# A long convolution and a spectral mix on one core: slot order and copying engines at the borders of pairs, a product from PSUM, and the place of one load

## The chip, the cores and the metric

The kernel runs on one core of a Trainium2 chip. The time is device time of one execution, in microseconds (us). Engines: TensorE (PE) multiplies matrices and writes to PSUM; VectorE (DVE) and ScalarE (ACT) compute on SBUF and PSUM and copy between them; GpSimd (POOL) here issues DMAs and clears memory; SyncE (SP) issues DMAs. PSUM has eight banks of 512 32-bit words a partition.

## What is computed

```python
def _attn_ref(x, h):                      # x: 8 x 5696 x 128, h: 5696 x 128
    L = 2 * S
    y = irfft(rfft(x, n=L, axis=1) * rfft(h, n=L, axis=0)[None], n=L, axis=1)[:, :S]
    return y

def _moe_ref(x, w_r, w_i, w_ch):          # x is y of above; w_r, w_i: 64 x 128 x 128
    X = rfft(x, axis=1)
    # the first 64 modes are multiplied by complex 128 x 128 matrices, the others are dropped
    u = x + irfft(Y, n=S, axis=1)
    return u + maximum(u @ w_ch, 0)
```

The result is 8 x 5696 x 128 in float32. The first function is a causal convolution along the sequence; the second mixes the channels of the 64 lowest modes, adds the result and ends in a channel matmul with relu.

## The kernel before, in words

A transform of length 2 x 5696 is taken apart as 64 x 178. The kernel has 90 frequencies k of the inner transform (NK), done four at a time: 23 **ticks** (NT), the last with two. The eight batches go in four **pairs** (NP, `g_` from 0 to 3). There are two blocks. Block one transforms, multiplies with the filter and transforms back half-way, writing `zscr` in HBM; it also sums the spectrum's 64 modes in PSUM bank 7 (`MB`). Block two reads `zscr` again (tiles ZT0 to ZT4), finishes the convolution, adds the mixed modes and writes the output.

A recorder (lines 21 to 121) keeps one list of instructions an engine, in the order of the Python code. Each engine runs its list in order, so the order of the code is the order of each queue; the recorder derives the semaphore waits from tokens such as `("bank", 3)`, `("as", 12)` or `("u", 0)`.

**Start.** PE first transforms the filter h in 16 tiles (lines 409 to 423). Between their matmuls stand fillers, which multiply the constant F1 with itself into banks 6 and 7 and whose result nobody reads: four behind each tile, twelve behind the last (line 416). DVE meanwhile spreads x into `x_sb` (named Xin; `x_place`, line 355).

**Tiles of x.** `a_tile(j)` (line 429), j from 0 to 31, is the first transform of one pair: four matmuls with F1 (128x180) into two banks (a **slot**, named by its first bank), then a copy of 128x720 into `a_sb` (As), by DVE or ACT. All 32 tiles must be copied before the next pair's first tick (`AST`, line 427). For pair 0 they run ahead of the ticks; for the others, tiles 0 to 6 stand in the last four ticks of the pair before (`border`, line 508, with slot and engine of each), and tiles 7 to 31 behind them (lines 633 and 634), in slots 2, 0, 4, 6 by a counter that runs on from pair to pair, the copies by DVE and ACT in turn. Eight fillers follow the last one (`keep`, line 636).

**Ticks.** `tick(g_, t)` (line 556), t from 0 to 25, has in this order: the Xin copies of the next pair on DVE (ticks in `XPLACE`, line 551); 16 matmuls of As with the twiddles M into slot 0 or 2, alternating by tick (lines 563 to 571); the product with the filter (`products`, line 535); the border's tiles; the issue on POOL of a load of x for the next pair, Xt (even ticks 2 to 16, line 576), which waits for U of that tick; with the U of two ticks before (LC), four matmuls with Wc, two ACT copies into Zs or Zt and the write to `zscr` on SP (lines 579 to 594); with the Z of three ticks before (LM), the sums of modes in bank 7 (matmuls with G, lines 595 to 610). In pair 0 a part of the filter's transform is in the tick too.

A product (line 547, DVE, 128x2048 into U) reads its spectrum either from a copy that ACT made (Xs, line 544), which takes 1.22 us on DVE, or straight from PSUM, which takes 2.28 us and holds the two banks until then. Line 542 chooses: in pairs 1 to 3 the ticks 2, 5, ... 20 read from PSUM.

Behind a pair's last tick, ACT copies the mode sums out of bank 7 in two pieces (XT, lines 628 to 631).

**Ahead of block two.** In pair 3, some ticks issue the loads of block two on POOL (`early`, line 509). Behind tick 21 (NT - 2) stand, in this order: ZT1 (two DMAs, which wait for writes to `zscr` through tick 14, `SLACK`), the constant IBs, a memset of a part of ZT1, ZT2, a memset of ZT2. Each waits also for the tick's U (`pace`). Behind the pair come WI, ZT3 and ZT4 with their memsets.

**Block two** (from line 648). PE needs IBs and C (the mixed modes) to finish its first tile. It takes the ZT tiles in turn; when one has been used, SP loads the next into it.

Of the kernel before, what the change touches and what calls it, by code (L numbers as in the profile page):

```python
# [4 lines left out]
P = 128  # L5
# [118 lines left out]
def bass_long_conv_fft__then__afno_spectral_mix_kernel(nc, x, h, moe_w_r, moe_w_i, moe_w_ch, out):  # L124
    B, S, D = x.shape
# [170 lines left out]
    def bank(i):  # L296
        return ("bank", i)
# [111 lines left out]
    for j in range(16):  # L409
        t = turns("h", [0, 2, 4])  # L410
        for i in range(4):
            d = 4 * j + i
            mm(pv(t + i // 2, (i % 2) * 2 * NK, [[1, 2 * NK]]),
               ap(hp_sb, 2 * J * HS, 0, P, d, [[HS, 2 * J]]), f1_sb[:, :], True, True,
               [("hz",), ("hp", d // DC), ("f1",)], [bank(t + i // 2)])
        for i in range(4 if j < 15 else 12):
            mm(pv(6 + i % 2, 0, [[1, 2 * NK]]), f1_sb[:, 0:P], f1_sb[:, :], True, True, [("f1",)], [bank(6 + i % 2)])
        evac(bass.AP(ah_sb, 4 * j, [[HW, P], [DH, 2 * NK], [2, 2], [1, 2]]),
             pv(t, 0, [[1, 2 * NK], [512, 2], [2 * NK, 2]]),
             [bank(t), bank(t + 1)], [("ah", j)], 1.0 / 64,  # L420
             eng="vector" if j % 4 == 3 else "scalar")
        if j % 2:
            x_place(j // 2, x_raw[j // 2], XR[j // 2])

    HP = [("hz",), ("hp", 0), ("hp", 1)]
    AHT = [("ah", j) for j in range(16)]
    AST = [("as", j) for j in range(32)]

    def a_tile(j, slots, eng=None):
        t = turns("s", slots) if len(slots) > 1 else slots[0]  # L430
        for i in range(4):
            d = 4 * j + i
            mm(pv(t + i // 2, (i % 2) * 2 * NK, [[1, 2 * NK]]),
               ap(x_sb, XW, 0, P, d, [[XS, 2 * J]]), f1_sb[:, :], True, True,
               XIN + XZ + [("f1",)], [bank(t + i // 2)])
        evac(bass.AP(a_sb, 4 * j, [[AW, P], [D, 2 * NK], [2, 2], [1, 2]]),
             pv(t, 0, [[1, 2 * NK], [512, 2], [2 * NK, 2]]),
             [bank(t), bank(t + 1)], [("as", j)], 1.0 / 64, eng=eng, after=once(("hp", j), HP))
# [63 lines left out]
    def load_s4(part):  # L502
# [2 lines left out]
            [("s4", part, 0)], after=pace + (AST if part else M_ALL[1:4]))  # L505

    V, A = "vector", "scalar"
    border = {NT - 1: [(0, 2, V)], NT: [(1, 0, V), (2, 2, A)], NT + 1: [(3, 0, V), (4, 2, A)], NT + 2: [(5, 0, V), (6, 2, V)]}
    early = {0: lambda: load_id(), 1: lambda: load_w(0), 3: lambda: load_w(1), 6: lambda: load_w(2), 8: lambda: load_w(3),
             12: lambda: load_s4(1), 16: lambda: load_s4(0),  # L510
             14: lambda: clear_zt(0),
             15: lambda: load_zt(0, "gpsimd"),
             NT - 2: lambda: (load_zt(1, "gpsimd", SLACK), load_ib(), clear_zt(1), load_zt(2, "gpsimd"), clear_zt(2))}
    pace = []
    SLACK = [("zd", NP - 1, s_) for s_ in range(NT - NZL)]

# [18 lines left out]
    def products(g_, t, sl):  # L535
        n = len(ticks[t])
        bk = [bank(sl), bank(sl + 1)]
        i = t % NU
        hv = bass.AP(h_sb, KT * t * D, [[2 * HW, P], [HW, 2], [0, 2], [1, n * D]])
        uv = bass.AP(u_s[i], 0, [[2048, P], [1024, 2], [512, 2], [1, n * D]])  # L540
        src = pv(sl, 0, [[0, 2], [512, 2], [1, n * D]])
        if t % 3 != 2 if g_ else t != NT - 4:
            e = turns("e", list(range(NXS)))
            evac(bass.AP(x_s[e], 0, [[1024, P], [512, 2], [1, n * D]]), pv(sl, 0, [[512, 2], [1, n * D]]), bk,
                 [("xs", e)], eng="scalar")
            src, bk = bass.AP(x_s[e], 0, [[1024, P], [0, 2], [512, 2], [1, n * D]]), [("xs", e)]
        R.add("vector", lambda e: e.tensor_tensor(uv, src, hv, MULT),  # L547
              bk + [("h", t, 0), ("h", t, 1, 0), ("h", t, 1, J)], [("u", i)])
# [7 lines left out]
    def tick(g_, t):  # L556
        if g_ + 1 < NP:
            for i in range(2 * XC):
                if t == XPLACE[g_ > 0][i]:
                    x_place(i, x_st[i], xtok(i))  # L560
        with_h = with_h_at(g_, t)
        if t < NT:
            sl = XSLOT[0] if with_h else XSLOT[(t + (g_ == 0)) % 2]
            for i, k in enumerate(ticks[t]):
                for r in range(2):
                    for b in range(2):
                        col = k * 3 * J + (J if r == 0 else 0) + b * J
                        mm(pv(sl + b, i * D, [[1, D]]),
                           ap(m_sb, MW, J * b, J, col, [[1, P]]),
                           ap(a_sb, AW, J * b, J, (2 * k + r) * D, [[1, D]]), r == 0, r == 1,  # L570
                           AST + mtok(k), [bank(sl + b)])
            products(g_, t, sl)
        if t in border and g_ + 1 < NP:
            for j, sl, e in border[t]:
                a_tile(j, [sl], e)
        if g_ + 1 < NP and t % 2 == 0 and 0 < t <= 4 * XC:
            i = t // 2 - 1
            x_load(g_ + 1, i, x_st[i], xtok(i), [("u", t % NU)] + AST)
        if LC <= t < NT + LC:
            s_ = t - LC  # L580
            n = len(ticks[s_])
            i, zi = s_ % NU, s_ % NZS[g_]
            zb = [turns("z", ZBANK) for b in range(2)]
            for b in range(2):
                for r in range(2):
                    mm(pv(zb[b], 0, [[1, n * D]]), (W1, W2)[r], u_s[i][:, r * 1024 + b * 512:r * 1024 + b * 512 + n * D],
                       r == 0, r == 1, [("u", i), ("wc",)], [bank(zb[b])])
                evac(bass.AP(z_s[zi], b * D, [[1024, P], [2 * D, n], [1, D]]),
                     pv(zb[b], 0, [[D, n], [1, D]]), [bank(zb[b])], [("zs", zi, b)], eng="scalar",
                     after=once(("zx", zi, b), Z_OLD) if zi >= NZ else ())  # L590
            zo = (g_ * NK + KT * s_) * P * 256
            dma("sync", bass.AP(zs, zo, [[256, P], [P * 256, n], [1, 256]]),
                bass.AP(z_s[zi], 0, [[1024, P], [256, n], [1, 256]]), "z",
                [("zs", zi, 0), ("zs", zi, 1)], [("zd", g_, s_)])
        if LM <= t < NT + LM:
            s_ = t - LM
            zi = s_ % NZS[g_]
            if s_ == 0:
                mm(pv(MB, 0, [[1, 2 * P]]), m_sb[ZR:P, 0:P], ap(f1_sb, 2 * NK, ZR, P - ZR, 0, [[0, 2], [1, P]]), True, False, [("f1",)] + mtok(0), [bank(MB)])
            for i, k in enumerate(ticks[s_]):  # L600
                for b in range(2):
                    if k % 2:
                        o, off, n, sl = pv(MB, b * P, [[1, P]]), (k + 1) // 2 * P, P, (k + 1) // 2
                    else:
                        ms, off = even[k]
                        n, sl = 2 * len(ms), 0
                        dims = [[M, 2]] if len(ms) == 1 else [[ms[1] - ms[0], 2], [M, 2]]
                        o = pv(MB, b * P + ms[0], dims)
                    mm(o, z_s[zi][:, i * 256 + b * P:i * 256 + b * P + P], g_sb[:, off:off + n],
                       False, k == NK - 1 and b == 1, [("g", sl // GP), ("zs", zi, b)], [bank(MB)])  # L610
        if with_h:
            filter_tick(t + LH, [2, 3])

# [5 lines left out]
    for g_ in range(NP):  # L619
        for t in range(NT + LM):  # L620
            tick(g_, t)
            if g_ == 0 and t < 2:
                keep(8, 4)
            assert g_ + 1 < NP or not wp
            if g_ == NP - 1 and t in early:
                pace[:] = [("u", min(t, NT - 1) % NU)]
                early[t]()
        evac(bass.AP(xt, 2 * g_ * XTW + M, [[B * XTW, P], [XTW, 2], [1, P]]), pv(MB, 0, [[P, 2], [1, P]]),
             [bank(MB)], [("xt", g_)], 1.0 / 64, eng="scalar", after=[("ag", k) for k in range(NS + 2 * XN, NK)])
        evac(bass.AP(xt, 2 * g_ * XTW, [[B * XTW, P], [XTW, 2], [1, M]]), pv(MB, M, [[P, 2], [1, M]]),  # L630
             [bank(MB)], [("xtn", g_)], -1.0 / 64, eng="vector" if g_ + 1 == NP else "scalar", after=[("ag", k) for k in range(NS + 2 * XN, NK)])
        if g_ + 1 < NP:
            for j in range(7, 32):
                a_tile(j, [2, 0, 4, 6])
                if j == 31:
                    keep(8, turns("s", [2, 0, 4, 6]))
                if wp and j % 2 == 1:
                    dst, src_, ring, tok = wp.pop(0)
                    dma("gpsimd", dst, src_, ring, (), [tok], after=[("as", j)])
# [192 lines left out]
```

## Time and profile before

| | us |
|---|---|
| median of three runs | 401.45 |
| the three runs | 401.30, 401.45, 403.42 |
| the profiled execution | 403.32 |
| its span | 401.1 |
| PE busy in the span | 374.8 (93%) |
| DVE busy | 313.8 (78%) |
| ACT busy | 299.2 (75%) |
| POOL busy | 82.8 (21%) |
| first ticks of pairs 0, 1, 2, 3 | at 46.27, 111.76, 171.55, 230.39 |
| last G matmuls of pair 3 | 273.67 |
| first matmuls with IBs | 285.24 |

How to read the views. A line of the timeline has the start and the time of a run of like instructions, in us from the start of the span, then engine, line, operation, what it writes and reads with the shape, and how many they are (x4); in brackets stands how long the engine was idle before, and what ended that. An instruction that overlaps the one before it shows its whole time, so back-to-back copies come closer than their times. A row of the table by windows has the bounds, the length and the busy time of PE, of PE's weight loads, DVE, ACT and POOL, each with its number of instructions; the last three columns are the granted clock of PE (1.00 is full speed), the share of the DMA engines and GB/s. In the chain of waits each line is a start, a time and what the end of the kernel waited for then. Many lines of code share a helper: line 320 is every matmul, 308 and 310 are ACT copies, 312 and 314 DVE copies, 317 every DMA.

### The profile page before, as it was taken

To read this page: it belongs to the slowest core of one execution; us is meant where nothing else is said; L and a number is where in the kernel's file an instruction comes from. 1 tells how busy PE (TensorE), PEld (TensorE's weight loads), DVE (VectorE), ACT (ScalarE), POOL (GpSimd) and SP (SyncE) were. 2 spreads that over 40 slices of the span, in tenths; PEclk is the share of its full clock that TensorE was granted. 3 is DMA by queue.
4 is the path that set the end of the run, shared out by engine and by line. 5 is a ranking of instruction groups with operands and counts; after the bars stand their busy time and mean duration, and the time that the engine had idled before them with its cause. 6 is when DMAs were issued, how large, how long until landed. Compare 5 with 4: busy or idle time off the path is not lost.

```text
span 401.1 us, 12515 instructions
## 1 busy us (share of the span) xinstructions
PE 374.8 (93%) x5388; PEld 285.6 (71%) x5388; DVE 313.8 (78%) x343; ACT 299.2 (75%) x478; POOL 82.8 (21%) x133
## 2 busy tenths in 40 slices
PE   7989899998989998989998989999899999999994
PEld 7978666666856665846666856667688889888873
DVE  6878788997979998979997978882335677677876
ACT  1358689997978886878887979986246767776785
POOL 8300022220733220733210411216700000000000
PEclk9998999999999999999999999999599999999998
DMA  8997469997999995999995849999999999999769
GB/s 156 189 303 276 130 118 292 269 259 228 98 145 178 262 246 148 99 132 186 252 231 160 83 144 328 325 315 303 405 391 395 379 412 412 413 408 375 310 253 357
DMA packets 86864, 103.94 MB, mean 259 GB/s; under 512 B 22638, under 2 KB 72430, under 8 KB 83330
## 3 DMA queue, kind: packets, MB, share of 16 engines
q1 hardware_dynamic: 62523, 67.73, 48.6%
q0 software_dynamic: 24288, 35.43, 42.5%
q8 instruction: 42, 0.69, 0.7%
q14 instruction: 11, 0.09, 0.1%
HBM read 70.61 MB, written 51.12 MB: 304 GB/s over the span
## 4 chain that ended last, share of the span: by engine, by line
PE 49%; DMA 18%; DVE 16%; ACT 6%; POOL 5%; issue 4%; DVEq 0%; POOLq 0%; SPq 0%
PE ps L320 49%; DVE U L547 8%; DMA Xt<-in_x_dram 5%; DVE As L314 5%; DMA Xr<-in_x_dram 4%; DMA ZT4b<-zscr 4%; DMA out_dram<-Os 3%; POOL Xr L317 2%; ACT Xs L308 2%; DMA Hs<-Hs 2%; ACT As L310 2%; DVE Hs L312 1%; ACT R L766 1%; DVE Xin L356 1%; ACT UT L308 1%
## 5 line engine op out<-in xcount | busy, mean ns | idle before, releaser
L547 DVE TENSOR_TENSOR U<-Xs,Hs 128x2048 f16<-128x2048 f16 x70 | 82.7, 1190 | 20.6 <-ACT Xs L308 20.3
L320 PE MATMUL ps<-U,Wc 128*128 128x512 f16 (+1 forms) x368 | 93.6, 377 | 1.9 <-DVE U L547 1.9
L308 ACT CAST Zs<-ps 128x512 f16<-128x512 f32 (+1 forms) x142 | 75.8, 594 | 9.8 <-PE ps L320 9.1
L308 ACT CAST Xs<-ps 128x1024 f16<-128x1024 f32 x70 | 69.5, 997 | 15.6 <-PE ps L320 14.8
L767 DVE TENSOR_TENSOR O<-ps,R 128x512 f32<-128x512 f32 x81 | 52.5, 686 | 19.5 <-ACT R L766 12.9
L314 DVE TENSOR_SCALAR As<-ps 128x720 f16<-128x720 f32 x68 | 57.7, 902 | 9.7 <-PE ps L320 9.2
L766 ACT ACTIVATE R<-ps 128x512 f32<-128x512 f32 x96 | 51.0, 574 | 14.6 <-PE ps L320 14.2
L320 PE MATMUL ps<-F,Xin 128*128 128x180 f16 x512 | 54.8, 254 | 6.8 <-DVE As L314 2.8
L320 PE MATMUL ps<-As,M 64*128 64x128 f16 x1440 | 56.0, 217 | 5.4 <-ACT Xs L308 2.0
L320 PEld LDWEIGHTS ps<-F,Xin 128*128 128x128 f16 x512 | 45.8, 155 | 14.4 <-DVE As L314 4.1
L310 ACT ACTIVATE As<-ps 128x720 f16<-128x720 f32 x60 | 46.3, 786 | 11.6 <-PE ps L320 10.6
L320 PE MATMUL ps<-WI,UT 128*128 128x256 f16 x360 | 51.9, 278 | 0.5 <-DVE O L767 0.4
L320 PEld LDWEIGHTS ps<-As,M 64*128 64x128 f16 x1440 | 40.7, 94 | 15.5 <-DVE U L547 3.3
L320 PEld LDWEIGHTS ps<-U,Wc 128*128 128x128 f16 x368 | 29.1, 98 | 31.5 <-DVE U L547 2.4
L547 DVE TENSOR_TENSOR U<-ps,Hs 128x2048 f16<-128x2048 f32 x22 | 50.2, 2284 | 0.9 <-DMA Hs<-Hs 0.9
L317 POOL DMA_DIRECT2D Xt<-in_x_dram x48 | 25.5, 535 | 110.9 <-PE ps L320 95.9
L308 ACT CAST UT<-ps 128x712 f16<-128x712 f32 x40 | 30.0, 752 | 21.1 <-PE ps L320 20.3
L320 PE MATMUL ps<-IBs,C 128*128 128x356 f16 x128 | 40.6, 327 | 2.1 <-DMA IBs<-cIB 1.3
L320 PEld LDWEIGHTS ps<-WI,UT 128*128 128x128 f16 x360 | 39.3, 152 | 4.2 <-issue 2.3
L320 PEld LDWEIGHTS ps<-G,Zs 128*128 128x128 f16 x556 | 28.1, 96 | 14.9
L320 PE MATMUL ps<-G,Zs 128*128 128x128 f16 (+2 forms) x556 | 34.3, 192 | 0.0
L320 PE MATMUL ps<-F 128*128 128x180 f16 (+1 forms) x272 | 28.2, 253 | 2.6 <-DMA F<-cF 2.6
(87 smaller groups left out, 489.2 us busy)
## 6 DMA issues: line engine op xcount, KB each, us to landing
out_dram<-O SPq DMA_DIRECT2D x39, 512.0 KB, 8.6
zscr<-Zs SPq DMA_DIRECT2D x68, 256.0 KB, 6.2
Xt<-in_x_dram POOLq DMA_DIRECT2D x24, 320.0 KB, 6.9
zscr<-Zt SPq DMA_DIRECT2D x20, 256.0 KB, 7.1
W<-wscr POOLq DMA_DIRECT2D x4, 1024.0 KB, 8.3
M<-cM POOLq DMA_DIRECT2D x5, 720.0 KB, 20.5
ZT0a<-zscr SPq DMA_DIRECT2D x3, 1024.0 KB, 9.8
Hs<-Hs SPq DMA_DIRECT2D x44, 64.0 KB, 6.2
```

Source lines behind the costliest of these rows:

```text
L308: R.add(e, lambda h_: h_.copy(dst, src), reads, writes, after=after)
L310: R.add(e, lambda h_: h_.activation(dst, src, COPY, scale=scale), reads, writes, after=after)
L312: R.add(e, lambda h_: h_.tensor_copy(dst, src), reads, writes, after=after)
L314: R.add(e, lambda h_: h_.tensor_scalar_mul(dst, src, scale), reads, writes, after=after)
L317: R.add(eng, lambda h_: h_.dma_start(dst, src), reads, writes, ring=ring, after=after)
L320: R.add("tensor", lambda h_: h_.matmul(o, l, r, start=st, stop=sp), reads, writes)
L356: R.add("vector", lambda e: e.tensor_copy(bass.AP(x_sb, i * XN * XS, [[XW, NQ], [XS, XN], [1, D]]), bass.AP(src, 0, [[XB, NQ], [D, XN], [1 ...
L547: R.add("vector", lambda e: e.tensor_tensor(uv, src, hv, MULT), bk + [("h", t, 0), ("h", t, 1, 0), ("h", t, 1, J)], [("u", i)])
L766: R.add("scalar", lambda e: e.activation(rv, src_r, RELU), bk, [("r", i % NR)], after=once(("r", i % NR), G_ALL + XTT + [("y", 0), ("y", 1 ...
L767: R.add("vector", lambda e: e.tensor_tensor(ov, src_u, rv, ADD), bk + [("r", i % NR)], [key + (h_,)], after=once(key, old))
```

## The change

- Behind the last tile of h, 30 fillers instead of 12.
- The border's tiles have other engines: tile 2 DVE instead of ACT, tile 3 ACT instead of DVE, tile 4 DVE instead of ACT, tile 6 ACT instead of DVE. The slots are as before.
- Where a tick has two of the border's tiles, the second stands behind the matmuls with Wc, the Z copies and the write of that tick instead of ahead of them; in tick 25, which has none of these, behind the sums of modes.
- Tiles 7 to 31 have slots 4, 6, 0, 2 in turn for every pair; odd ones are copied by DVE, even ones by ACT, and of the last one DVE copies one bank and ACT the other (`"both"`, with a token of its own). The eight fillers have slot 6.
- In pairs 1 to 3 the products that read from PSUM are those of ticks 0, 3, ... 18 instead of 2, 5, ... 20: seven, as before.
- Behind tick 21 of pair 3 POOL's order is IBs, ZT1, ZT2, then the memsets of ZT1 and ZT2.

```diff
-        for i in range(4 if j < 15 else 12):
+        for i in range(4 if j < 15 else 30):
...
-    AST = [("as", j) for j in range(32)]
+    AST = [("as", j) for j in range(33)]
...
+        if eng == "both":
+            for i, e in enumerate(("vector", "scalar")):
+                evac(bass.AP(a_sb, 4 * j + 2 * i, [[AW, P], [D, 2 * NK], [1, 2]]), pv(t + i, 0, [[1, 2 * NK], [2 * NK, 2]]),
+                     [bank(t + i)], [("as", j + i)], 1.0 / 64, eng=e, after=once(("hp", j), HP))
+            return
...
-    border = {NT - 1: [(0, 2, V)], NT: [(1, 0, V), (2, 2, A)], NT + 1: [(3, 0, V), (4, 2, A)], NT + 2: [(5, 0, V), (6, 2, V)]}
+    border = {NT - 1: [(0, 2, V)], NT: [(1, 0, V), (2, 2, V)], NT + 1: [(3, 0, A), (4, 2, V)], NT + 2: [(5, 0, V), (6, 2, A)]}
...
-             NT - 2: lambda: (load_zt(1, "gpsimd", SLACK), load_ib(), clear_zt(1), load_zt(2, "gpsimd"), clear_zt(2))}
+             NT - 2: lambda: (load_ib(), load_zt(1, "gpsimd", SLACK), load_zt(2, "gpsimd"), clear_zt(1), clear_zt(2))}
...
-        if t % 3 != 2 if g_ else t != NT - 4:
+        if t % 3 or t > NT - 4 if g_ else t != NT - 4:
...
-        if t in border and g_ + 1 < NP:
-            for j, sl, e in border[t]:
-                a_tile(j, [sl], e)
+        drain = list(border[t]) if t in border and g_ + 1 < NP else []
+        if drain:
+            j, sl, e = drain.pop(0)
+            a_tile(j, [sl], e)
...
+            if drain:
+                j, sl, e = drain.pop(0)
+                a_tile(j, [sl], e)
...
+        if drain:
+            j, sl, e = drain.pop(0)
+            a_tile(j, [sl], e)
...
-                a_tile(j, [2, 0, 4, 6])
+                a_tile(j, [(4, 6, 0, 2)[(j - 7) % 4]], "both" if j == 31 else V if j % 2 else A)
                 if j == 31:
-                    keep(8, turns("s", [2, 0, 4, 6]))
+                    keep(8, 6)
```

## The prediction

> **What bounds the kernel now.** I read the page's forty slices first, then the chain of waits, then the timeline at each place that the diff touches. TensorE (PE) is 93% busy, so most of the kernel runs at its pace; its idle time and its granted clock are what an edit can change.
>
> ```profile
> PE   7989899998989998989998989999899999999994
> PEclk9998999999999999999999999999599999999998
> ```
>
> The clock row shows two dips: slice 28 (280.8 us on) and, smaller, slice 3. The PE timeline has what lies ahead of slice 3's, and the table by windows (PE busy first, granted clock third from the end) shows the dip itself:
>
> ```profile
> 24.95 1.09 PE L320 MATMUL ps<-F 128*128 128x180 f16 x12
> 27.78 1.16 PE L320 MATMUL ps<-F,Xin 128*128 128x180 f16 x12 [1.74 <-DVE Xin L356]
> ```
> ```profile
> 26.27:29.68 3.41, 1.65 (x17) 1.43 (x18) 2.04 (x3) 1.32 (x2) 0.00 (x0) 1.00 1.01 414
> 29.68:33.09 3.41, 3.41 (x24) 3.26 (x24) 2.61 (x3) 1.84 (x4) 0.00 (x0) 0.50 1.02 423
> 111.60:115.01 3.41, 2.01 (x51) 1.50 (x51) 1.56 (x3) 2.03 (x3) 1.07 (x2) 1.00 1.74 173
> 173.04:176.45 3.41, 2.53 (x38) 1.42 (x39) 3.19 (x3) 2.37 (x5) 0.06 (x1) 1.00 1.13 110
> 231.07:234.48 3.41, 2.11 (x41) 1.11 (x36) 2.38 (x3) 2.37 (x3) 0.00 (x0) 1.00 0.00 0
> ```
>
> A stretch with PE busy for 1.65 of 3.41 us (48%) is followed by 3.4 us at half clock. The last three rows are the starts of pairs 1, 2 and 3: 59%, 74% and 62% busy, and no dip after them. So the limit lies somewhere between 48% and 59%, and the starts of pairs stand not far above it.
>
> At a border (pair 2 to 3 here) the 32 tiles of x go through copies on VectorE (DVE) and ScalarE (ACT), which end together; PE waits for them:
>
> ```profile
> 214.89 0.54 PE L320 MATMUL ps<-F,Xin 128*128 128x180 f16 x4 [0.43 <-DVE As L314]
> 215.27 1.03 PE L320 MATMUL ps<-U,Wc 128*128 128x512 f16 x4
> 215.47 0.77 ACT L310 ACTIVATE As<-ps 128x720 f16<-128x720 f32 x1 [0.99 <-PE ps L320]
> 216.46 0.80 PE L320 MATMUL ps<-F,Xin 128*128 128x180 f16 x8
> 216.99 0.91 DVE L314 TENSOR_SCALAR As<-ps 128x720 f16<-128x720 f32 x1 [1.34 <-PE ps L320]
> 219.01 0.55 ACT L310 ACTIVATE XT<-ps 128x256 f16<-128x256 f32 x2 [0.40 <-PE ps L320]
> ```
>
> Tile 2 waits in PE's queue ahead of U,Wc matmuls that were ready: DVE then idles 1.34 us. Back to back, a copy takes 0.837 us on DVE (14 in 11.72) and 0.789 on ACT (13 in 10.26).
>
> The start of a pair:
>
> ```profile
> 230.39 1.07 PE L320 MATMUL ps<-As,M 64*128 64x128 f16 x32
> 232.12 0.62 PE L320 MATMUL ps<-As,M 64*128 64x128 f16 x16 [0.66 <-ACT Xs L308]
> 233.38 1.04 PE L320 MATMUL ps<-U,Wc 128*128 128x512 f16 x4 [0.64 <-DVE U L547]
> 236.72 0.62 PE L320 MATMUL ps<-As,M 64*128 64x128 f16 x16
> ```
>
> Last, block two: the load of IBs is held on POOL behind ZT1a, and PE waits 1.29 us for it at 285.24; soon after, PE reaches ZT4b's landing (301.36 in the chain):
>
> ```profile
> 273.77 0.53 POOL L317 DMA_DIRECT2D ZT1a<-zscr  x1 [11.01 <-PE ps L320]
> 274.81 1.23 POOL L317 DMA_DIRECT2D IBs<-cIB  x1
> 284.94 16.37 DMA ZT4b<-zscr
> ```
>
> **The change part by part.** The profiled execution took 403.32 us, its span 401.1; the median of the runs is 401.45, 1.87 less. I sum changes against the profiled execution and then add the sum to the median.
>
> *18 more fillers.* Twelve take 1.09 us, some 0.08 each, so 30 end near 27.45, under the Xin copy that PE waits for until 27.73: they cost nothing. They lift the stretch from 26.27 to 29.68 above 75% busy, and the dip should go. In it four tile matmuls take 0.60 us; without it three slots and two copying engines allow some 0.42 a tile, and tile 11's copy, at 34.3, would start near 33.1. **-1.2 us** (0 in executions that had no such dip; the 1.87 us between profile and median may be one).
>
> *Borders.* With t from the last pair's rows: tile 1 at 213.97 as now, then U,Wc at 214.33 (they need U, done at 213.42), tile 2 at 215.19, its DVE copy 215.77 to 216.67; tile 3's ACT copy 216.48 to 217.26; tile 4 at 216.72, DVE copy 217.30 to 218.20; tile 6 at 218.25, ACT copy 218.83 to 219.61. So the drain itself is tighter. But the two XT copies now queue behind tile 6's on ACT, until 220.16 (now 219.56), and tile 8 sits in banks 6 and 7, of which 7 is what XT is copied from: PE, in order, holds tile 8's last two matmuls until 220.2 and tile 9 behind them. DVE resumes with tile 9 near 220.94, ACT with tile 8 near 220.63. From there DVE has 11 copies by 0.837 and a half (estimated 0.47, from 0.90 for the whole), to 230.61; ACT 12 by 0.789 and a half (0.43), to 230.5. Now: 230.33. **+0.3** at this border; **+0.55** at the first (tile 0 shares its bank there with tick 22, which moves tile 2 by 0.27); **-0.55** at the second, where now tile 7 waits for XT and DVE has one tile more (17.27 us from the first DVE copy to the next pair's first matmuls, against 16.45 at the others). Together **+0.3** (-1 to +1.5).
>
> *First product from PSUM.* Call the end of the copies E (230.33 now). Now U0 runs from a copy: ACT 231.05, DVE 232.10, done about E+2.97. From PSUM (2.28 us) it starts at E+0.72 and is done at E+3.0: the same. But bank 0 is now held until E+3.0, so tick 2's matmuls move from E+1.79 to E+3.05, and tick 3's after them. Now U2 is the long one and holds tick 4 to 236.72, E+6.39; then U3 would, without harm. Tick 5 comes at E+8.42 against E+8.24: **+0.18** at each of three starts, **+0.5**.
>
> *What that does to the clock.* PE would be busy from E+0.06 to E+1.13, idle to E+3.05 and busy after. A stretch of 3.41 us that begins between E-0.85 and E+1.35 is then under 48% busy, as the one at 26.27 was; now none is under 55%. If such stretches follow each other at a fixed spacing with no tie to the kernel, as the edges of the two dips, 29.68 and 278.85, suggest (73.0 times 3.413 us apart), 2.2 of 3.41 positions hit, two starts in three. Half clock for 3.41 us of ticks that PE paces (1.847 us a tick from tick 5 to tick 21) costs half of that, 1.7 us. Nothing wins it back: DVE fills ticks 9 to 21 as well. **+3.4** for two (0 to +5.1).
>
> *Order of the long products in pairs 1 and 2.* Long ones move from ticks 11, 14, 17, 20 to 9, 12, 15, 18, where an Xin copy (0.60 back to back) stands ahead of each. Each then releases its bank some 0.3 late for PE; against that, tick 22 no longer waits 0.62 for U20. DVE's work is the same. But the eighth Xt load is issued after U16, which ends at 204.56 instead of 203.22: by the issue before it (0.53 after U14, a second piece 0.52 on, landing 6.85 later) it lands near 212.4, where DVE wants it at 211.66. Landings range from 3.4 to 8.2 us, median 6.4. I take **+0.5** for each of two pairs (0.15 to 1.4), **+1.0**.
>
> *End of pair 3.* Three ACT copies in a row (ticks 19 to 21) instead of a gap at tick 20: tick 21's starts 0.1 to 0.2 late, **+0.2**.
>
> *IBs first.* POOL is free at 262.76 and U21 ends at 271.46: issue at 272.0 instead of 274.81, and the landing (10.3 us then) before 283.3, when C is ready. PE's 1.29 us go. ZT1 keeps its time, ZT2 goes 3 us earlier, ZT3 and ZT4 1.0 (memset and IBs off their way). What is late next is ZT4b: DMA shares are near 1.0 from 277 on, at 412 GB/s, so only the gaps ahead (some 0.75 us at 273 and 0.4 at 276) can be filled: **-1.0** (0 to -3.0; -3.0 if PE led: 1.29 and the 1.7 of a half-clock stretch, 285.68 to 289.09, that its 62% busy predecessor caused).
>
> Sum: -1.2 +0.3 +0.5 +3.4 +1.0 +0.2 -1.0 = +3.2: 406.5 for the profiled execution, **404.5** beside the median.
>
> On the clock the Trainium skill ("TensorE: Matmul & The Clock Gate", Part 1, What's actually happening, and Why this matters for your kernels) says that half rate follows an idle window of some 3.4 us, on a free-running window, and warns of gaps over about 3 us. The trace bears out the window's length and fixed spacing, not the full idle window: a gap of 1.74 us was enough. By the page's rule a gap of 1.9 us is harmless, and the sum would be that of the first rival.
>
> **Rivals.** *No dip at the starts.* For it: three starts at 59% to 74% stayed at full clock, and the limit is known from one stretch alone. Against it: 48% and a gap of 1.74 us sufficed at 26 us. The sum without it is -0.2: 401.3 (400 to 402.5).
> *Faster: block two is led by PE, not by DMA.* If ZT4b lands 2 to 3 us earlier (ZT2 is issued 3 us earlier), IBs is worth 3.0 and, with no dip at the starts, the sum is -2.2; with the Xt load in time and borders at -1, -4: 398.5 (397 to 399.4). It decides as soon as ZT4b lands before 298.5. Against it: DMA shares of 1.0.
> *Slower still: three dips and the Xt load 1.4 late in both pairs*: +6.7: 408. That needs a landing over 7.5 us.
>
> **Numbers.** Forecast 0.46 (403 to 406.5), no dip 0.24, faster 0.20, slower still 0.10. The range 399.0 to 407.0 leaves out about half of the faster and most of the last. Within 0.5% (2 us, about what a measurement of this kernel tells from no change) lie the no-dip case and a little of the forecast: 0.27; faster 0.21; slower 0.52.
>
> **What would show it.** Fillers: clock 1.00 from 28 to 34 us, tile 11's copy 1.2 us earlier. Borders: XT before tile 8, DVE idle about 1 us before tile 9. Starts: PE idle 1.9 us ahead of tick 2, then 3.4 us at 0.50 at one to three of them. Xt: a DVE wait on the load ahead of the last Xin copy. IBs: no PE wait on IBs, and a wait on ZT4b in its place. I am wrong if the clock holds at the starts or if PE passes ZT4b without a wait.

## The result, and the profile after

The changed kernel takes 407.59 us in the median (406.77 to 408.16, four runs) against 402.24 (401.30 to 403.42, four runs): a ratio of 1.013, with a 95% interval from 1.009 to 1.017. It is slower, as forecast, by 5.35 us where 3.2 were summed, and 0.6 us above the range. The profiled execution took 408.16 us, its span is 406.1, 5.0 more than before.

The slices of the profile's page, as shown for the kernel before:

```profile
PE   7999899997979998979999979999999999999994
PEclk9999999999989999999999989999599999999998
```

Slice 3 is whole again; slices 11 and 23, counted from 0 and 10.15 us long each (112 and 233 us on), have dips that were not there, at 115.59 and 238.47 us by the clock's record, 36 times 3.413 us apart. Their place is that of the starts of pairs 1 and 3. The table by windows, cut at 115.59 and at whole multiples of 3.413 us from it, PE's busy time first and the granted clock third from the end:

```profile
26.84:30.25 3.41, 2.76 (x31) 2.31 (x30) 2.00 (x3) 1.44 (x2) 0.00 (x0) 1.00 1.01 421
112.18:115.59 3.41, 1.47 (x45) 1.16 (x40) 3.04 (x2) 1.04 (x2) 0.86 (x2) 1.00 1.63 159
115.59:119.00 3.41, 3.41 (x23) 1.39 (x22) 2.36 (x3) 2.05 (x3) 0.61 (x2) 0.50 0.23 37
173.62:177.03 3.41, 1.85 (x43) 1.48 (x40) 2.60 (x3) 1.93 (x3) 2.20 (x3) 1.00 1.51 147
177.03:180.44 3.41, 2.82 (x40) 1.52 (x40) 2.78 (x3) 2.09 (x4) 0.00 (x0) 1.00 0.83 84
235.06:238.47 3.41, 1.47 (x31) 0.91 (x26) 3.34 (x2) 1.50 (x2) 0.00 (x0) 1.00 0.02 5
238.47:241.88 3.41, 3.41 (x23) 1.20 (x20) 2.85 (x2) 2.09 (x4) 0.55 (x1) 0.50 0.50 98
```

At pairs 1 and 3 the gap lies inside one window, which has PE busy for 43%, and the next window runs at half clock. At pair 2 the same gap is cut by an edge at 177.03 (54% and 83%), and the clock holds. The gap itself, in PE's timeline at the start of pair 1, and the Wc matmuls at half clock behind it (1.79 us for four instead of 1.04):

```profile
111.88 1.07 PE L320 MATMUL ps<-As,M 64*128 64x128 f16 x32 [0.21 <-ACT As L310]
114.89 0.62 PE L320 MATMUL ps<-As,M 64*128 64x128 f16 x16 [1.94 <-DVE U L552]
115.45 1.79 PE L320 MATMUL ps<-U,Wc 128*128 128x512 f16 x4
```

At the borders, here DVE's copies of the first one, the drain has no idle of 1.34 us any more, but one of 0.79 us ahead of tile 9: PE stands idle for 0.84 us behind the XT copies before it can go on with the tiles:

```profile
101.49 2.55 PE L320 MATMUL ps<-F,Xin 128*128 128x180 f16 x26 [0.84 <-ACT XT L310]
98.68 2.76 DVE L314 TENSOR_SCALAR As<-ps 128x720 f16<-128x720 f32 x3 [0.63 <-PE ps L320]
102.22 9.52 DVE L314 TENSOR_SCALAR As<-ps 128x720 f16<-128x720 f32 x12 [0.79 <-PE ps L320]
```

The eighth load of Xt in pair 1, in the chain of waits: its issue starts at 147.38, behind U16, its second piece lands at 155.77, and DVE has been free since 154.38:

```profile
146.90 0.48 issue
147.38 0.50 POOL Xt L317
147.88 7.89 DMA Xt<-in_x_dram
155.77 0.02 issue
155.79 0.70 DVE Xin L356
```

Ahead of block two POOL now issues IBs first, and PE no longer waits for it:

```profile
277.37 0.53 POOL L317 DMA_DIRECT2D IBs<-cIB  x1 [8.79 <-DVE U L552]
278.87 0.53 POOL L317 DMA_DIRECT2D ZT1a<-zscr  x1 [0.97 <-DMA zscr<-Zt]
```

To place the difference I cut both profiles at events that both have: the first matmuls of each pair, the first DVE copy of each border, ACT's last XT copy, the first matmuls with IBs.

| stage, us | before | after | difference |
|---|---|---|---|
| start to pair 0's first tick | 46.27 | 45.55 | -0.72 |
| pair 0 to its first border copy | 49.04 | 48.96 | -0.08 |
| border 0 | 16.45 | 17.37 | +0.92 |
| pair 1 to its first border copy | 42.52 | 46.26 | +3.74 |
| border 1 | 17.27 | 16.47 | -0.80 |
| pair 2 to its first border copy | 42.39 | 43.32 | +0.93 |
| border 2 | 16.45 | 16.39 | -0.06 |
| pair 3 to ACT's last XT copy | 43.91 | 45.82 | +1.91 |
| XT to the first IBs matmuls | 10.94 | 9.98 | -0.96 |
| from there to the end of the span | 115.86 | 115.98 | +0.12 |

The borders cancel, the loads and the fillers gain 1.7, and the loss of 6.6 lies in the ticks of pairs 1 to 3, whose only edit is where the products read from PSUM.

### The profile page after: what moved, and what is told of

Same layout as the page of the kernel before. It is cut to its first block, busy times and chain, and to the rows that moved or that the text cites. A ratio compares the mean times of both kernels' runs of the same rounds, so it can differ in the third digit from the quotient of the medians.

```text
span 406.1 us, 12559 instructions
## 1 busy us (share of the span) xinstructions
PE 377.6 (93%) x5406; PEld 286.9 (71%) x5406; DVE 316.0 (78%) x345; ACT 299.0 (74%) x479; POOL 84.1 (21%) x133
## 3 DMA queue, kind: packets, MB, share of 16 engines
q1 hardware_dynamic: 62523, 67.73, 47.8%
## 4 chain that ended last, share of the span: by engine, by line
PE 65%; DVE 12%; DMA 8%; ACT 8%; issue 5%; POOL 2%; DVEq 0%; POOLq 0%
PE ps L320 64%; DVE U L552 6%; DMA Xr<-in_x_dram 4%; DMA Xt<-in_x_dram 4%; ACT Xs L308 2%; DVE Xin L356 2%; POOL Xr L317 2%; ACT As L310 2%; DVE As L314 2%; ACT R L778 1%; ACT UT L308 1%; DVE Hs L312 1%; ACT Zs L308 1%; DVE UT L312 0%; ACT XT L310 0%
## 5 line engine op out<-in xcount | busy, mean ns | idle before, releaser
L320 PE MATMUL ps<-U,Wc 128*128 128x512 f16 (+1 forms) x368 | 95.9, 384 | 0.0
L310 ACT ACTIVATE As<-ps 128x720 f16<-128x720 f32 (+1 forms) x61 | 45.9, 770 | 11.6 <-PE ps L320 10.8
L317 POOL DMA_DIRECT2D Xt<-in_x_dram x48 | 26.9, 564 | 114.1 <-PE ps L320 90.9
L320 PE MATMUL ps<-F 128*128 128x180 f16 (+1 forms) x290 | 30.0, 254 | 2.6 <-DMA F<-cF 2.6
```

Source lines behind the costliest of these rows:

```text
L310: R.add(e, lambda h_: h_.activation(dst, src, COPY, scale=scale), reads, writes, after=after)
L317: R.add(eng, lambda h_: h_.dma_start(dst, src), reads, writes, ring=ring, after=after)
L320: R.add("tensor", lambda h_: h_.matmul(o, l, r, start=st, stop=sp), reads, writes)
```

## The experiments

The theory: the products from PSUM hold the whole loss, by three ways: the gap at the starts pulls the clock down; the long products beside Xin copies make PE and DVE wait for each other; the eighth Xt load comes late. The rivals: the borders' new order or the load order costs the time; the dips have nothing to do with the gap. Of the runs around the products and the slots the table gives the ratio to the kernel before in its own group, and the stages of its profile; the time to pair 0's first tick and pair 0's ticks differ from profile to profile, also on one chip (45.5 to 47.5 us, and 47.8 to 51.0), and are left out.

| kernel | ratio (95%) | dips at starts | pairs 1, 2, 3 | borders 0, 1, 2 |
|---|---|---|---|---|
| before | 1 | none | 42.52, 42.39, 43.91 | 16.45, 17.27, 16.45 |
| after | 1.013 (1.009 to 1.017) | 1, 3 | 46.26, 43.32, 45.82 | 17.37, 16.47, 16.39 |
| after, again | 1.014 (1.010 to 1.019) | 2 | 43.31, 45.96, 44.25 | 17.28, 16.37, 16.47 |
| fillers at the starts | 1.011 (1.006 to 1.016) | none | 43.32, 44.80, 44.25 | 17.29, 16.36, 16.47 |
| the same, Xt one tick earlier | 1.0045 (1.001 to 1.0075) | none | 43.31, 43.31, 44.25 | 17.28, 16.36, 16.36 |
| products put back | 0.990 (0.984 to 0.9955) | none | 42.17, 42.05, 43.77 | 16.84, 16.48, 16.47 |
| only the start moved | 1.0055 (1.002 to 1.009) | 1, 2 | 44.26, 44.64, 44.15 | 17.38, 16.46, 16.48 |
| only the later products moved | 0.998 (0.994 to 1.001) | none | 44.06, 44.04, 43.88 | 16.60, 16.48, 16.48 |
| put back, slots 4, 0, 2, 6 | 0.990 (0.986 to 0.993) | none | 42.55, 42.19, 43.78 | 16.06, 15.87, 15.87 |
| the same, Xt one tick earlier | 0.992 (0.989 to 0.996) | none | 41.79, 41.80, 43.77 | 16.69, 15.89, 15.89 |

**The products put back.**

```diff
-        if t % 3 or t > NT - 4 if g_ else t != NT - 4:
+        if t % 3 != 2 if g_ else t != NT - 4:
```


> The changed kernel with the products from PSUM put back to ticks 2, 5, ... 20; all else as changed. By my sum from the two profiles the products hold the whole loss: starts 3 x 0.2, dips 2 x 1.7, order of the long products and the late Xt load 2.3, end of pair 3 0.2, so 6 to 6.5 us come back and it ends at 401 to 402, a little under the kernel before. If the borders or the load order were to blame, it stays above 405.

Measured: 400.38 us, ratio 0.990, faster than the kernel before. Pairs 1 and 2 are back at 42.1, no dips at starts. The products hold the whole loss; borders and loads do not cause it.

**Only the start, only the rest.** The ticks that read from PSUM in pairs 1 to 3:

```diff
-        if t % 3 or t > NT - 4 if g_ else t != NT - 4:
+        if t not in (0, 5, 8, 11, 14, 17, 20) if g_ else t != NT - 4:
```


> The changed kernel with products from PSUM in ticks 0, 5, 8, 11, 14, 17, 20 of pairs 1 to 3: only the first has moved. It should have the 1.9 us gap and dips at some starts, but no late Xt load and no 0.25 us waits of PE in ticks 11 to 20: 403.5 to 406, by the number of dips. If the order of the long products costs nothing, it stays at 407 to 408; if the start costs nothing, 401 to 402.

```diff
-        if t % 3 or t > NT - 4 if g_ else t != NT - 4:
+        if t not in (2, 4, 6, 9, 12, 15, 18) if g_ else t != NT - 4:
```


> The changed kernel with products from PSUM in ticks 2, 4, 6, 9, 12, 15, 18 of pairs 1 to 3: the first tick goes through a copy again, the later ones are as changed. No dips at the starts; the DVE wait on the eighth Xt load (1.4 and 0.3 us) and PE's four waits of 0.25 us in pairs 1 and 2 stay: 403 to 404.5. If only the start matters, 401 to 402; if only the order, 407.

Measured: 405.70 and 403.75 us, against 400.38 for neither. The first has the gap and dips at two of three starts; DVE waits for Xt for 0.49 and 0.86 us, where it was 0.64 and 0.51 in the kernel before. Its pair 3, without a dip, is 0.38 over the kernel with the products put back: the price of the start itself. The second has no dip; its pairs 1 and 2 are 1.9 and 2.0 longer, and DVE waits 1.2 and 1.5 us for Xt in them. Both ways are real and separate: 5.3 and 3.4 us, together 8.7. The changed kernel was not run in this group; by the ratios to the kernel before it stands 2.3 to 2.4%, 9 to 10 us, above the kernel with the products put back, and by the pairs of its first profile 7.4 us.

**Fillers in the gap.**

```diff
             if g_ == 0 and t < 2:
                 keep(8, 4)
+            if g_ and t == 1:
+                keep(22, 4)
```


> The changed kernel with 22 fillers (F1 by F1, some 0.08 us each, 1.7 us) between ticks 1 and 2 of pairs 1 to 3, in banks 4 and 5, where PE now stands idle for 1.94 us; the wait itself stays. If the gap is what pulls the granted clock down, both dips (115 and 238 us) go, and the time falls by 1.7 us a dip, that is by 2 to 5 us from 407.6, to some 403 to 405. If the dips have another cause, or cost nothing, it stays at 407 to 408 with the dips.

The timeline of PE at the start of pair 1, and a stretch of 3.41 us that holds it:

```profile
114.09 1.07 PE L320 MATMUL ps<-As,M 64*128 64x128 f16 x32 [0.20 <-ACT As L310]
115.09 1.88 PE L320 MATMUL ps<-F 128*128 128x180 f16 x22
117.10 0.62 PE L320 MATMUL ps<-As,M 64*128 64x128 f16 x16
```
```profile
114.09:117.50 3.41, 3.28 (x68) 2.96 (x70) 2.75 (x2) 1.01 (x1) 1.16 (x2) 1.00 1.60 161
```

Tick 2 comes as late as before (3.01 us behind the first tick's matmuls), yet there is no dip at any start, here or in the kernel below that has the Xt loads earlier on top of the fillers: none of six, where five of nine unfilled gaps had one (two profiles of the changed kernel, one with only the start moved). Pair 3, which has no load of Xt, takes 44.25 instead of 45.82. So the gap pulls the clock down, and a dip costs 1.6 us. The time moved less than expected: 407.28, a ratio of 1.011 whose interval overlaps that of the changed kernel, so the gain is shown by the stages alone. In this profile the Xt load is 1.9 us late in pair 2.

**The changed kernel once more.** No edit.


> The changed kernel unaltered, once more, as the base of this group. If a dip needs the gap to meet a fixed spacing of stretches that has no tie to the kernel, the dips stand at other starts than in the first profile (one to three of the three), each worth 1.7 us in its pair, and the waits on the eighth Xt load differ as well (0 to 2 us). If dips belong to certain pairs, they are at pairs 1 and 3 again.

Measured: 407.93 us, ratio 1.014. Now there is one dip, at pair 2, and its Xt wait (1.5 us) is in pair 2 too; pairs 1 and 3 have neither. So neither belongs to a certain pair. The late load does not come from the dip: with the fillers, and with only the later products moved, it is late without one.

**Xt one tick earlier**, on top of the fillers:

```diff
-        if g_ + 1 < NP and t % 2 == 0 and 0 < t <= 4 * XC:
-            i = t // 2 - 1
+        if g_ + 1 < NP and t % 2 == (g_ > 0) and 0 < t <= 4 * XC - (g_ > 0) :
+            i = (t + (g_ > 0)) // 2 - 1
```


> The changed kernel with the fillers between ticks 1 and 2, and with the Xt loads of pairs 1 and 2 issued one tick earlier (odd ticks 1 to 15). No dip at a start, no DVE wait on Xt: pairs 1 and 2 from first tick to first border copy 43.2 us each, which is 1.1 over the 42.1 of the kernel with the products put back, the part that belongs to the early start (0.4) and the long products beside Xin copies (0.7) alone. Time 2 to 4 us under the changed kernel of this group. If Xt was not the cause of the waits, they stay, 44 to 46.

Measured: 404.27 us, ratio 1.0045, clear of the changed kernel's 1.014 in the same group. No wait on Xt is left and pairs 1 and 2 take 43.31 each. The kernel to hold this against is the last one below, which also has the loads early but the products put back: 41.79 and 41.80. Of the 1.5 us more, 0.4 is the start. The other 1.1 belongs to long products beside Xin copies: PE waits four times, 1.05 us in all, for their banks. The second and third of these waits in pair 1:

```profile
138.58 0.62 PE L320 MATMUL ps<-As,M 64*128 64x128 f16 x16 [0.25 <-DVE U L552]
144.44 0.62 PE L320 MATMUL ps<-As,M 64*128 64x128 f16 x16 [0.25 <-DVE U L552]
```

**The products alone**, on the kernel before:

```diff
-        if t % 3 != 2 if g_ else t != NT - 4:
+        if t % 3 or t > NT - 4 if g_ else t != NT - 4:
```


> The kernel before with nothing changed but the products from PSUM, now in ticks 0, 3, ... 18. If they hold the whole loss: 6 us slower than before, 1.5% (starts 0.4 and bursts 0.8 in pairs 1 and 2, Xt waits 0 to 2, one to three dips of 1.7). If the borders' other order is needed for the loss, less than 2 us.

Measured: 406.26 us, ratio 1.009 (1.004 to 1.013). Its profiled execution (412.2 us) lies far above its median, so its trace isn't used. So there is a loss without the borders' new order. But it is 3.6 us (1.8 to 5.2 by the interval), less than the 6 expected and than what the changed kernel loses over the one with the products put back; why is not shown.

**The other three parts alone**, on the kernel before: 30 fillers; IBs first; the borders with their slots and engines (that diff is the change without the three lines of fillers, products and loads).

```diff
-        for i in range(4 if j < 15 else 12):
+        for i in range(4 if j < 15 else 30):
...
-             NT - 2: lambda: (load_zt(1, "gpsimd", SLACK), load_ib(), clear_zt(1), load_zt(2, "gpsimd"), clear_zt(2))}
+             NT - 2: lambda: (load_ib(), load_zt(1, "gpsimd", SLACK), load_zt(2, "gpsimd"), clear_zt(1), clear_zt(2))}
```


> The kernel before with 30 instead of 12 fillers behind the last tile of h. If the dip at 29 us comes from the gap of 1.74 us, it is gone where the last Xin copy is as early as in the first profile, and pair 0's first tick comes 0.7 us earlier; on a chip where the first loads of x land later a gap and a dip can remain. Time 0 to 0.7 us under the kernel before; if the dip has another cause it stays and nothing changes.

> The kernel before with the new order of loads on POOL alone. From the last XT copy to the first matmul with IBs 9.5 to 10.1 us instead of 10.94, no PE wait on IBs, and the wait on ZT4b as late as before or gone: 0.8 to 1.0 us less. If block two is led by PE alone, up to 3 us less; if by the DMA rate alone, nothing.

> The kernel before with the new borders alone (engines, places, slots 4, 6, 0, 2, the last tile by both engines). Borders of 16.5 to 17.3, 16.4 and 16.4 us where 16.45, 17.27 and 16.45 were: in sum 0 to -0.8, the time within 0.5% of the kernel before. If the drain's new order were a gain by itself, all three would be under 16.4.

Measured: ratios 1.0008 (0.997 to 1.005), 1.0007 (0.997 to 1.004) and 1.0008 (0.9975 to 1.004). None can be told from no change by the time. Nor do they add up to the 0.990 that all three had together with the products put back (0.984 to 0.9955, four runs); that is not explained. The profiles have the stages as expected: no dip at 29 us with the fillers; 9.56 us from XT to IBs, and no wait on IBs; borders of 17.10, 16.49 and 16.47. The fillers are no sure cure: in the profile of the kernel with fillers at the starts and early Xt, the last Xin copy came 1 us later than in the changed kernel's first profile, PE stood idle for 1.41 us, and a dip followed at 30 us. And in the profile of the fillers alone there is a dip elsewhere, at 91.56 us in pair 0's ticks, behind a window with two idle times of PE, 0.97 and 1.09 us:

```profile
88.15:91.56 3.41, 1.57 (x12) 0.63 (x12) 2.94 (x2) 1.99 (x3) 0.00 (x0) 1.00 0.96 261
91.56:94.97 3.41, 3.21 (x28) 1.81 (x28) 3.41 (x5) 2.94 (x5) 0.00 (x0) 0.50 0.95 282
```

**Slots 4, 0, 2, 6**, with the products put back:

```diff
-                a_tile(j, [(4, 6, 0, 2)[(j - 7) % 4]], "both" if j == 31 else V if j % 2 else A)
+                a_tile(j, [(4, 0, 2, 6)[(j - 7) % 4]], "both" if j == 31 else V if j % 2 else A)
                 if j == 31:
-                    keep(8, 6)
+                    keep(8, 0)
```


> The changed kernel with the products put back and slots 4, 0, 2, 6 in turn for tiles 7 to 31, so that the tile in bank 7 comes two tiles later and does not wait for XT. The borders take 16.5 to 17.3 us in the changed kernel; with DVE's idle 0.8 us ahead of tile 9 gone they should take 15.8 to 16.5, 0.5 to 0.8 us less each: 399 or 1 us under the kernel with products put back, and the fastest so far. If the copies' own pace sets the border, the wait is only moved and the borders stay at 16.4.

DVE's copies of the last border; the idle time ahead of tile 9 is 0.19 instead of 0.79:

```profile
217.39 2.76 DVE L314 TENSOR_SCALAR As<-ps 128x720 f16<-128x720 f32 x3 [0.63 <-PE ps L320]
220.35 9.51 DVE L314 TENSOR_SCALAR As<-ps 128x720 f16<-128x720 f32 x12 [0.19 <-PE ps L320]
```

Measured: 398.18 us, ratio 0.990; borders of 16.06, 15.87 and 15.87, 0.6 to 0.8 less each. So the wait on XT was the price of the slot order. The time does not tell this kernel from the one with the products put back: that had a ratio of 0.990 too.

**The same with Xt one tick earlier.**


> The kernel with the products put back and slots 4, 0, 2, 6, and in addition the Xt loads of pairs 1 and 2 issued one tick earlier. In the kernel without this DVE waits 0.5 and 0.3 us for Xt, so 0.3 to 0.8 us less than its 398.2, the fastest yet; if those waits lie in DVE idle time that PE's bank waits cause anyway, no difference.

Measured: 397.31 us, ratio 0.992 (0.989 to 0.996). Pairs 1 and 2 take 41.8 each, without a wait on Xt. Both of these versions beat both kernels by the time; between the two it does not decide.

## Why the prediction was right and where it was wrong

| term | forecast | in the first profile |
|---|---|---|
| fillers behind h | -1.2 | -0.72 |
| borders | +0.3 | +0.06 |
| starts, three | +0.5 | +1.1 (0.38 each, from the start moved alone) |
| dips, two | +3.4 | +3.1 (1.57 in pair 3, taken for both) |
| order of the long products and Xt, pairs 1 and 2 | +1.0 | +2.3 (pair 1 +1.8, pair 2 +0.55: what start and dip leave) |
| end of pair 3 | +0.2 | 0.0 |
| IBs first | -1.0 | -0.84 |
| sum | +3.2 | +5.0 |

**Right.** Each mechanism came as worked out. The first product from PSUM is ready no sooner and holds its bank 1.3 us longer; PE's gap was 1.94 us (1.92 forecast, E+1.13 to E+3.05); two of three starts fell to half clock, as the forecast took it. That it was two here is in part luck: the second profile of the same kernel has one, at another start. The borders came out at +0.9, -0.8 and -0.1, forecast +0.55, -0.55 and +0.3. DVE does wait for the eighth Xt load.

**Wrong: the size of the step "Order of the long products in pairs 1 and 2"**, +1.0 for the two pairs (0.15 to 1.4 each), where they paid 2.3. The step names two costs, and by its own figures they come to 1.3 a pair if they add: four releases 0.3 late less the 0.62 for U20 make 0.6, and a load that lands near 212.4 where DVE wants it at 211.66 makes 0.7. I took 0.5 a pair and gave no reason for less than the sum. The runs show that they add: in pair 1 PE waits 1.05 us at the banks and then 1.51 us behind the Xin copy of the late load.

The banks came out about as figured: pairs without a late load take 43.31, which is 0.4 to 0.5 over the kernel before once the start is taken off. (The 1.1 found above is larger because the kernel before waits too: DVE for Xt, 0.64 and 0.51 us, and PE at tick 22 for U20, 0.69 and 0.55; where the loads are early and the products put back, both waits are gone.) The load missed both ways: in pair 1 it landed 7.89 us from the second piece's issue instead of 6.85 and cost 1.4, in pair 2 DVE waited 0.31 us for it, which cost nothing. In the four profiles with this order and these loads the waits range from none to 1.9 us, so this part is luck in a single execution. (The median of the landings in the profile before, given as 6.4, is 5.9.)

Not all of the distance to the forecast is the change's. Of the 3.1 us between 404.5 and 407.59, 0.8 lies in the kernel before, whose median is 402.24 here and was 401.45 when the sum was added to it.

**Smaller misses.** The starts were 0.38 each, not 0.18. The initial dip was worth 0.72, not 1.2: with three slots the copies, at full clock, did not come as close as 0.42 a tile (0.47 from tile 3 to tile 11). "What is late next is ZT4b" did not hold, and this was one of the signs of being wrong that the prediction named: ZT4b landed at 305.38, PE first used it at 305.43, without a wait; PE ran at half clock until 293. But block two gained no more for it: by the first output tile PE had won some 0.8 us more, and by the end it had lost that again. The slices there show the DMA engines at 400 GB/s and more, as before; that they took it back was not tried.

**The rivals.** "No dip at the starts" fell: five of nine. "Faster" fell. "Slower still" (408) was the nearest in time, but with two dips instead of three, and with the load 1.4 late in one pair instead of two.

Left open: what exactly the clock goes by. With windows cut at the dips' recorded edges, the five gaps of 1.94 us that a dip followed lie inside one window, with PE busy for 41% or 43% of it. The four without a dip are cut by an edge, one of them by only 0.02 us (only the start moved, pair 3; 44%). But the busy share in this view gives no limit: elsewhere dips followed windows of 46%, 48% and 51%, and ahead of block two the clock falls in every profile, in the changed kernel's first one behind a window of 98%.

## What to carry to other kernels

A product that skips a copy by reading PSUM is not faster if it ends at the same time and keeps the bank longer; look at who waits for the bank. Where an edit brings PE's idle times closer together, check the granted clock behind them, and if the wait can't be removed, fill it. When a long instruction is moved along a queue, move the timing of every load that hangs on its neighbours with it: here, one tick earlier for the Xt loads took the whole wait away.

## What the runs showed of the hardware

A gap of 1.94 us in PE's work is enough for 3.41 us at half clock, if it lies inside one window of a grid of 3.41 us (five of five); the same gap cut by an edge of the grid left the clock at full speed (four of four). Within a profile the dips begin whole windows apart. The grid has no tie to the kernel: reckoned back from the dips, its first edge lies 1.0, 1.7, 2.4 and 3.0 us behind the start of the span (products put back, only the start moved, before, after). The Trainium skill ("TensorE: Matmul & The Clock Gate", Part 1, What's actually happening) has the window's 3.41 us and that it runs freely, which these traces bear out; that a whole window must be idle they do not. Fillers that nobody reads count as work for the clock: with 22 of them in the gap it held six times of six.
